# One PSUM pool with single 2-bank slots, mixed chunk sizes, and side work placed at fractions of each pass

## The chip, the cores and the metric

The kernel runs on one core of a Trainium2 chip. The metric is device time in microseconds; the time before is the median of three runs, 275.36 us (274.27 to 275.84). A profile of one execution (275.36 us, span 273.3 us) is shown beside it. Engines are named as in the profile: PE (matrix engine), PEld (its weight loads), DVE (vector), ACT (scalar), POOL (the engine whose queue starts the input loads here), SP (the queue of the output stores).

## The reference

```python
for _ in range(5):                      # P: [batch, head, 8, 8]
    P = exp(P - max(P)); P = P / sum(P, axis=-1); P = P / sum(P, axis=-2)
k_sorted = einsum('bhij,bhjcd->bhicd', P, k_blocks)     # blocks of 96 tokens
v_sorted = einsum('bhij,bhjcd->bhicd', P, v_blocks)
attn = softmax(scale * q_block @ k_sorted_block.T)      # inside each block
x = (attn @ v_sorted_block), heads side by side         # 3072 tokens x 512
g = x @ w_gate; val = x @ w_val                         # 512 -> 1536
out = (g * sigmoid(g) * val) @ w_out                    # 1536 -> 512
```

There are 4 batches, 8 heads, 768 tokens (8 blocks of 96), head size 64.

## The kernel before

**Mixing.** The 8x8 mixing matrices of all heads are made first (L177 to L201). A block-diagonal matrix per batch, `rmix`, mixes k over the blocks and passes q through an identity, so one pair of matmuls per token position c mixes k and moves q (`kq_chunk`, L217; `kq_wide`, L406, for batch 0). The result lies in PSUM as `tkq` and is drained to `kqt`, transposed. v is first copied to `vch` (L107) and mixed per head column (`v_chunk` L229, `v_wide` L421, and `v_pair_chunk` L240 for batches 2 and 3 at once); `tv` is drained to `vt`. `drain` (L202) copies on DVE ("v") or ACT ("s").

**Units.** One unit is half of the blocks of one head pair: `qk` (L253) computes scores and their exp, `av` (L273) multiplies by v, takes the reciprocal of the sum and scales (`r_sb`, `st`), `xtr` (L291) transposes to `x_ps` and copies to `xt`, the feed-forward's input. A batch has eight units, four per half.

**Feed-forward.** There are 8 passes n of 384 tokens each (half a batch). For each of 12 columns m, `gate` (L306) does four matmuls, a tanh on ACT (`th_sb`) and a vector step (`gs_sb`), `value` (L321) four matmuls and a vector step (`h`). `outp` (L332) multiplies h of the pass before by `wo_sb`, in three parts of four matmuls, then a copy and a store by SP. `gate`, `value` and `outp` all take their PSUM bank under the tag `gen`.

**PSUM.** The prologue has a pool `wide` (L65): three 2-bank slots wa, wb, wc, one bank wd for warm-up matmuls and one bank we. After the first half of batch 0 it is closed, and a second pool opens (L458): `gen` with 3 banks, `att` with 3 banks (shared by qk, tkq, tv and x_ps), `av` with one 2-bank slot.

**What sets the order.** On PE and POOL the order is the program's own (a manual schedule); in the prologue also on DVE and ACT. After the prologue a scheduler orders DVE and ACT. `merge` (L480) interleaves a pass (`ffn`, L496) with side work (units of this or the next batch, mixing of the next batch): after each step of the pass it places side steps in proportion to costs that are written by hand, so that the side work is through at 0.85 of the pass. In a pass with k/q mixing the units come first and six double chunks of 8+8 columns follow them.

**Loads.** All inputs come through POOL's queue in this order: v, q and k of batch 0, six pairs of gate and value weights of 256 columns (`load_gv`, L103), k, q and v of batch 1, `wo_sb`; after the copies of batch 1's v, the loads of batches 2 and 3 (L506 to L513).

Of the kernel before, what the change touches and what calls it, by code (L numbers as in the profile page):

```python
# [17 lines left out]
def kernel(  # L18
# [46 lines left out]
    wide = tc.tile_pool(name="wide", bufs=1, space=bass.MemoryType.PSUM)  # L65
    psum = wide.__enter__()
# [67 lines left out]
    for m in range(0, DF, 256):  # L134
        load_gv(m, m + 256)
    load_k(1, 0, C)
    load_q(1, 0, C)
    load_v(1, 0, C)
# [31 lines left out]
    def pair_tile(name, slot):  # L170
        return psum.tile([128, 1024], FP32, name=name, tag=slot)

    def bank_tile(name, slot):
        return psum.tile([128, 512], FP32, name=name, tag=slot)

    p_ps = pair_tile("p_ps", "wa")[0:BH, 0:NB * NB].rearrange("p (i j) -> p i j", j=NB)
# [40 lines left out]
    def kq_chunk(b, cb, eng, tag):  # L217
        nat = kq_tiles[b]
        dst = kqt_tile(b).rearrange("p (n c) -> p n c", c=C)
        rm = rmix[b].rearrange("p two a g i -> p two (a g i)")  # L220
        tp = psum.tile([128, 8, 2 * GI], FP32, name="tkq", tag=tag)
        for lc in range(8):
            for two in range(2):
                nc.tensor.matmul(tp[two * D:(two + 1) * D, lc, :],  # L224
                                 lhsT=nat[:, cb * 8 + lc, :],
                                 rhs=rm[:, two, :], start=True, stop=True)
        drain(eng, dst[:, :, ts(cb, 8)], tp.transpose([0, 2, 1]))

    def v_chunk(b, db, eng, tag):  # L229
        rows = highr if b % 2 else lowr  # L230
        dst = vt_tile(b // 2)[:, b % 2]
        mix = vmix[b // 2][rows, b % 2].rearrange("p a b -> p (a b)")
        tp = psum.tile([128, 8, H * NB], FP32, name="tv", tag=tag)
        for ld in range(8):
            at = (db * 8 + ld) * C
            nc.tensor.matmul(tp[:, ld, :], lhsT=vch[rows, at:at + 128], rhs=mix,  # L236
                             start=True, stop=True)
        drain(eng, dst[:, :, ts(db, 8)], tp[0:C].transpose([0, 2, 1]))

    def v_pair_chunk(pair, db, eng, tag):  # L240
        dst = vt_tile(pair).rearrange("p u n e -> p (u n) e")
        mix = vmix[pair].rearrange("p u a b -> p (u a b)")
        tp = psum.tile([128, 4, 2 * H * NB], FP32, name="tv", tag=tag)
        for ld in range(4):
            at = (db * 4 + ld) * C
            nc.tensor.matmul(tp[:, ld, :], lhsT=vch[:, at:at + 128], rhs=mix,  # L246
                             start=True, stop=True)
        drain(eng, dst[:, :, ts(db, 4)], tp[0:C].transpose([0, 2, 1]))
# [4 lines left out]
    def qk(b, u):  # L253
        half, g = divmod(u, H2)
        flat = kqts[b]
        pss = [psum.tile([128, 4, C], FP32, name=f"qk{two}", tag="att") for two in range(2)]
        for i4 in range(4):
            at = (g * NB + half * 4 + i4) * C
            for two in range(2):
                lo = two * D  # L260
                nc.tensor.matmul(pss[two][:, i4, :], lhsT=flat[lo:lo + D, at:at + 128],  # L261
                                 rhs=flat[lo:lo + D, GI * C + at:GI * C + at + C],
                                 start=True, stop=True)
        mine = []
        for two in range(2):
            e = e_all[:, ecount[0] % 8, :]
            ecount[0] += 1
            nc.scalar.activation(e[:, 0:4 * C], pss[two][0:C].rearrange("p a c -> p (a c)"),  # L268
                                 AF.Exp, scale=scale)
            mine.append(e)  # L270
        es[(b, u)] = mine

    def av(b, u, tag="av"):  # L273
        half, g = divmod(u, H2)
        vt = vts[b // 2][:, b % 2].rearrange("p (h i) e -> p h i e", h=H)
        av_ps = psum.tile([128, 2, 512], FP32, name="av_ps", tag=tag, bufs=1)
# [14 lines left out]
    def xtr(b, u, eng, tag="att"):  # L291
# [4 lines left out]
        x_ps = psum.tile([128, 4, C], BF16, name="x_ps", tag=tag, bufs=1 if tag == "we" else 3)  # L296
# [3 lines left out]
        drain(eng, xts[(b, half)][:, g, :], x_ps.rearrange("p a b -> p (a b)"))  # L300
# [5 lines left out]
    def gate(n, m):  # L306
        xt = xts[divmod(n, 2)]
        if m == 0:
            h_tiles[n] = hpool.tile([128, NFC, TW], BF16, name=f"h{n}", tag="h")
        g_ps = psum.tile([128, TW], FP32, name="g_ps", tag="gen")  # L310
        for kc in range(NKC):
            nc.tensor.matmul(g_ps, lhsT=wg_sb[:, kc, ts(m, 128)], rhs=xt[:, kc, :],  # L312
                             start=(kc == 0), stop=(kc == NKC - 1))
        th_sb = gsp.tile([128, TW], BF16, name="th_sb", tag="th")
# [6 lines left out]
    def value(n, m):  # L321
        xt = xts[divmod(n, 2)]
        v_ps = psum.tile([128, TW], FP32, name="v_ps", tag="gen")
        for kc in range(NKC):
            nc.tensor.matmul(v_ps, lhsT=wv_sb[:, kc, ts(m, 128)], rhs=xt[:, kc, :],  # L325
                             start=(kc == 0), stop=(kc == NKC - 1))
        nc.vector.scalar_tensor_tensor(h_tiles[n][:, m, :], v_ps, 0.5, gs_tiles.pop(m),  # L327
# [4 lines left out]
    def outp(n, t3, part):  # L332
        b, half = divmod(n, 2)
        h_w = h_tiles[n]
        if part == 0:
            o_tiles[n] = psum.tile([128, DM], FP32, name="o_ps", tag="gen")
# [11 lines left out]
    idle_ps = bank_tile("idle_ps", "wd")  # L348

    def fill(n, width=512):  # L350
        for _ in range(n):
            nc.tensor.matmul(idle_ps[:, 0:width], lhsT=warm_sb[:, 0:128], rhs=warm_sb[:, 0:width],
                             start=True, stop=True)

    for _ in range(84):
# [3 lines left out]
                     rhs=v_tiles[0][lowr, HC:HC + 2, :].rearrange("p c d -> p (c d)"),  # L359
                     start=True, stop=True)  # L360
    fill(9)

    w_ps = bank_tile("w_ps", "we").rearrange("p (s i b h) -> p s i b h", s=2, b=B, h=H)

    def weights(half):
        for i in range(NB):
            nc.tensor.matmul(w_ps[half * R:(half + 1) * R, half, i].rearrange("p b h -> p (b h)"),
# [6 lines left out]
    def mix_of(b):  # L374
# [5 lines left out]
            w_ps[lo:lo + R, b % 2, :, b].transpose([0, 2, 1]), op=ALU.mult)  # L380
# [3 lines left out]
            w_ps[0:R, 0, :, b].rearrange("p i (g two) -> p two g i", two=2), op=ALU.mult)  # L384

    def qk_wide(u):
        half, g = divmod(u, H2)
        flat = kqts[0]
        ps = pair_tile("qk", ["wa", "wb", "wc", "wc"][u]).rearrange("p (two n) -> p two n", two=2)
        for i4 in range(4):  # L390
            at = (g * NB + half * 4 + i4) * C
            for two in range(2):
                lo = two * D
                nc.tensor.matmul(ps[:, two, i4 * C:(i4 + 1) * C], lhsT=flat[lo:lo + D, at:at + 128],
                                 rhs=flat[lo:lo + D, GI * C + at:GI * C + at + C],
                                 start=True, stop=True)
        n = ecount[0] % 8
        ecount[0] += 2
        nc.scalar.activation(e_all[:, n:n + 2, 0:4 * C], ps[0:C, :, 0:4 * C], AF.Exp, scale=scale)  # L399
        es[(0, u)] = [e_all[:, n, :], e_all[:, n + 1, :]]  # L400

    mix_of(0)
    kdst = kqt_tile(0).rearrange("p (n c) -> p n c", c=C)
    rm = rmix[0].rearrange("p two a g i -> p two (a g i)")

    def kq_wide(cb, engs, slot):  # L406
        tp = pair_tile("tkq", slot).rearrange("p (l n) -> p l n", n=2 * GI)
        for lc in range(16):
            for two in range(2):
                nc.tensor.matmul(tp[two * D:(two + 1) * D, lc, :],  # L410
                                 lhsT=kq_tiles[0][:, cb * 16 + lc, :],
                                 rhs=rm[:, two, :], start=True, stop=True)
        w = 16 // len(engs)
        for n, eng in enumerate(engs):
            drain(eng, kdst[:, :, cb * 16 + n * w:cb * 16 + (n + 1) * w],
                  tp[:, n * w:(n + 1) * w].transpose([0, 2, 1]))

    vdst = vt_tile(0)[:, 0]
    vm = vmix[0][lowr, 0].rearrange("p a b -> p (a b)")

    def v_wide(db, eng, slot):  # L421
        tp = pair_tile("tv", slot).rearrange("p (l n) -> p l n", n=H * NB)
        for ld in range(16):
            at = (db * 16 + ld) * C
            nc.tensor.matmul(tp[:, ld, :], lhsT=vch[lowr, at:at + 128], rhs=vm,
                             start=True, stop=True)
        drain(eng, vdst[:, :, ts(db, 16)], tp[0:C].transpose([0, 2, 1]))

    for b in range(1, B):
        mix_of(b)  # L430
    slots = ["wa", "wb", "wc"]
    for n in range(4):
        v_wide(n, "s", slots[2 * n % 3])
        kq_wide(n, "v", slots[(2 * n + 1) % 3])
    kq_wide(4, "s", slots[8 % 3])
    kq_wide(5, "sv", slots[9 % 3])
    fill(3)
    qk_wide(0)
    qk_wide(1)
    qk_wide(2)  # L440
    av(0, 0, "wa")
    av(0, 1, "wb")
    xtr(0, 0, "s", "we")
    av(0, 2, "wa")
    qk_wide(3)
    fill(1)
    xtr(0, 1, "s", "we")
    av(0, 3, "wb")
    fill(1)
    xtr(0, 2, "s", "we")  # L450
    fill(2)
    xtr(0, 3, "s", "we")
    fill(2)
# [3 lines left out]
    wide.__exit__(None, None, None)  # L457
    psum = ctx.enter_context(tc.tile_pool(name="psum", bufs=3, space=bass.MemoryType.PSUM))  # L458
    man = tc.manual_schedule(engines={ET.PE, ET.Pool})
    man.__enter__()  # L460

    def units(b, us):
        todo = []
        us = list(us)
        for n in range(len(us) + 2):
            if n < len(us):
                todo.append((0.27, lambda u=us[n]: qk(b, u)))
# [92 lines left out]
```

The softmax here doesn't subtract the row's maximum and nothing guards it: scores larger than these inputs give would overflow.

## Time and profile before

| what | value |
|---|---|
| median of three runs | 275.36 us |
| profiled execution | 275.36 us |
| its span | 273.3 us |
| PE, DVE, ACT busy | 254.0, 163.8, 125.9 us |
| first group of pass 0 starts | 29.64 us |
| last output matmul group ends | 269.3 us |

The difference of 2.06 us between time and span lies around the profiled instructions. Page section 2 cuts the span into 40 slices of 6.8 us; a digit is the busy share in tenths. A table of stretches gives busy time and instruction count of each engine, then the mean clock granted to PE (1.00 is full), the DMA engines' share and GB/s. The waits list says which engine stood idle before which line, and for whom: total, count, longest.

### The profile page before, as it was taken

The numbers are of one execution on the slowest core, as the hardware profiler recorded it, in microseconds if no ns is written. First come the engines' busy times: TensorE is split into PE (matmuls) and PEld (weight loads), VectorE is DVE, ScalarE is ACT, GpSimd is POOL, SyncE is SP. The second block draws the span as 40 slices with busy tenths as digits, with TensorE's granted clock in tenths as the row PEclk, the third lists the DMA queues.
The fourth block names the chain that finished last, engine by engine and source line by source line (L and its number), as shares of the span: only waits on it lengthen the run. The fifth ranks groups of instructions, "written<-read, shape, count | busy, mean of one in ns | idle before, by whom it ended". The sixth has DMA issues, their size and how long they took to land.

```text
span 273.3 us, 6511 instructions
## 1 busy us (share of the span) xinstructions
PE 254.0 (93%) x2775; PEld 147.0 (54%) x2775; DVE 163.8 (60%) x362; ACT 125.9 (46%) x242; POOL 47.2 (17%) x46
## 2 busy tenths in 40 slices
PE   3786984999998999999999999999999999999994
PEld 3374452665555556556655556555555555555541
DVE  6685493675369488456359487466566766566500
ACT  3876631446752534439963435335332534323311
POOL 7766300793029300000000000000000000000000
PEclk9998898899999999999999999999999999999998
DMA  6979999909996101101101101101110111011122
GB/s 114 209 98 171 197 224 200 183 4 193 210 232 138 41 1 41 41 2 38 41 0 42 38 0 41 41 4 38 41 38 2 38 38 41 1 41 38 40 77 77
DMA packets 12700, 20.86 MB, mean 76 GB/s; under 512 B 896, under 2 KB 8576, under 8 KB 12032
## 3 DMA queue, kind: packets, MB, share of 16 engines
q0 software_dynamic: 9168, 14.16, 29.4%
q1 hardware_dynamic: 3504, 6.30, 6.2%
q8 instruction: 21, 0.34, 0.5%
q14 instruction: 7, 0.06, 0.1%
HBM read 28.32 MB, written 6.29 MB: 127 GB/s over the span
## 4 chain that ended last, share of the span: by engine, by line
PE 78%; DMA 13%; DVE 3%; POOL 3%; issue 1%; ACT 1%; ACTq 0%; POOLq 0%
PE o_ps L339 23%; PE v_ps L325 22%; PE g_ps L312 21%; DMA kq<-in_q_dram 6%; PE tkq L224 4%; DMA kq<-in_k_dram 4%; DMA wv_sb<-in_moe_w_val_dram 3%; PE qk L261 2%; PE av_ps L281 2%; PE x_ps L298 1%; PE tv L246 1%; PE tv L236 1%; DVE h L327 1%; DVE gs_sb L317 1%; POOL wg_sb L101 1%
## 5 line engine op out<-in xcount | busy, mean ns | idle before, releaser
L317 DVE SCALAR_TENSOR_TENSOR gs_sb<-th_sb,g_ps 128x384 bf16<-128x384 bf16 x96 | 53.0, 552 | 64.0 <-ACT th_sb L315 62.4
L312 PE MATMUL g_ps<-xt,wg_sb 128*128 128x384 bf16 x384 | 78.9, 328 | 0.1
L325 PE MATMUL v_ps<-xt,wv_sb 128*128 128x384 bf16 x384 | 78.9, 328 | 0.0
L315 ACT ACTIVATE th_sb<-g_ps 128x384 bf16<-128x384 f32 x96 | 47.5, 495 | 58.2 <-PE g_ps L312 57.3
L339 PE MATMUL o_ps<-wo_sb,h 128*128 128x512 bf16 x288 | 68.6, 379 | 0.0
L327 DVE SCALAR_TENSOR_TENSOR h<-v_ps,gs_sb 128x384 bf16<-128x384 f32 x96 | 53.3, 555 | 7.8 <-PE v_ps L325 0.6
L312 PEld LDWEIGHTS <-wg_sb 128*128 128x128 bf16 x384 | 34.7, 98 | 22.8 <-issue 1.4
L325 PEld LDWEIGHTS <-wv_sb 128*128 128x128 bf16 x384 | 34.0, 98 | 20.3 <-issue 0.3
L339 PEld LDWEIGHTS <-h 128*128 128x128 bf16 x288 | 26.5, 98 | 27.5
L344 ACT COPY o_sb<-o_ps 128x512 f32<-128x512 f32 x24 | 14.1, 587 | 54.4 <-PE o_ps L339 54.3
L114 POOL COPY vch<-v 64x1536 bf16<-64x1536 bf16 (+1 forms) x10 | 28.0, 2856 | 33.4 <-DMA v<-in_v_dram 33.4
L268 ACT ACTIVATE e_all<-qk 96x384 bf16<-96x384 f32 x56 | 24.3, 488 | 5.7 <-PE qk L261 5.6
L206 ACT CAST vt<-tv 96x512 bf16<-96x512 f32 (+1 forms) x28 | 21.8, 808 | 6.5 <-PE tv L236 3.4
L204 DVE CAST kqt<-tkq 128x512 bf16<-128x512 f32 (+1 forms) x23 | 17.9, 778 | 8.2 <-PE tkq L224 6.4
L287 DVE TENSOR_TENSOR st<-av_ps,r_sb 96x512 bf16<-96x512 f32 x32 | 21.9, 684 | 0.7
L206 ACT CAST kqt<-tkq 128x512 bf16<-128x512 f32 (+1 forms) x20 | 12.1, 604 | 11.4 <-PE tkq L224 10.7
L224 PE MATMUL tkq<-rmix,kq 128*64 128x64 bf16 x576 | 12.9, 200 | 3.6 <-DMA kq<-in_q_dram 3.6
L224 PEld LDWEIGHTS <-kq 128*64 128x64 bf16 x576 | 10.9, 115 | 9.8 <-issue 9.8
L281 PEld LDWEIGHTS <-e_all 96*128 96x128 bf16 x256 | 12.0, 99 | 7.5 <-ACT e_all L399 1.7
L281 PE MATMUL av_ps<-vt,e_all 96*128 96x65 bf16 x256 | 13.7, 195 | 2.0 <-ACT e_all L399 1.2
L298 PEld LDWEIGHTS <-st 96*128 96x128 bf16 x128 | 8.9, 100 | 8.1 <-DVE st L287 3.7
L298 PE MATMUL x_ps<-ident,st 96*128 96x96 bf16 x128 | 11.2, 211 | 2.1 <-DVE st L287 2.1
(59 smaller groups left out, 121.8 us busy)
## 6 DMA issues: line engine op xcount, KB each, us to landing
out_dram<-o_sb SPq DMA_DIRECT2D x24, 256.0 KB, 2.0
kq<-in_q_dram POOLq DMA_DIRECT2D x4, 768.0 KB, 13.2
kq<-in_k_dram POOLq DMA_DIRECT2D x3, 768.0 KB, 13.1
v<-in_v_dram POOLq DMA_DIRECT2D x3, 768.0 KB, 17.7
wg_sb<-in_moe_w_gate_dram POOLq DMA_DIRECT2D x6, 256.0 KB, 9.5
wv_sb<-in_moe_w_val_dram POOLq DMA_DIRECT2D x6, 256.0 KB, 10.0
wo_sb<-in_moe_w_out_dram POOLq DMA_DIRECT2D x1, 1536.0 KB, 24.2
v<-in_v_dram POOLq DMA_DIRECT2D x2, 384.0 KB, 5.6
```

Source lines behind the costliest of these rows:

```text
L114: eng.tensor_copy(dst, src.transpose([0, 2, 1]))
L206: nc.scalar.copy(dst, src)
L224: nc.tensor.matmul(tp[two * D:(two + 1) * D, lc, :], lhsT=nat[:, cb * 8 + lc, :], rhs=rm[:, two, :], start=True, stop=True)
L268: nc.scalar.activation(e[:, 0:4 * C], pss[two][0:C].rearrange("p a c -> p (a c)"), AF.Exp, scale=scale)
L281: nc.tensor.matmul(o[:, two, i4, :], lhsT=e[:, i4 * C:i4 * C + 128], rhs=vt[:, 2 * g + two, half * 4 + i4, :], start=True, stop=True)
L298: nc.tensor.transpose(x_ps[:, i4, :], st[:, i4].rearrange("p a b -> p (a b)"), ident[0:C, 0:C])
L312: nc.tensor.matmul(g_ps, lhsT=wg_sb[:, kc, ts(m, 128)], rhs=xt[:, kc, :], start=(kc == 0), stop=(kc == NKC - 1))
L315: nc.scalar.activation(th_sb, g_ps, AF.Tanh, scale=0.5)
L317: nc.vector.scalar_tensor_tensor(gs_sb, th_sb, 1.0, g_ps, op0=ALU.add, op1=ALU.mult)
L325: nc.tensor.matmul(v_ps, lhsT=wv_sb[:, kc, ts(m, 128)], rhs=xt[:, kc, :], start=(kc == 0), stop=(kc == NKC - 1))
L327: nc.vector.scalar_tensor_tensor(h_tiles[n][:, m, :], v_ps, 0.5, gs_tiles.pop(m), op0=ALU.mult, op1=ALU.mult)
L339: nc.tensor.matmul(o_ps, lhsT=h_w[:, m, ts(t3, 128)], rhs=wo_sb[:, m, :], start=(m == 0), stop=(m == NFC - 1))
```

## The change

The two pools become one of fixed slots: `gen` with 3 banks, `a` and `b` with one 2-bank slot each, `x` with one bank. `av` takes `a`; `qk`, `kq_chunk`, `v_chunk` and `v_pair_chunk` take `b` after the prologue; `x_ps` takes `x`. Chunks take a start and a size: 16 k/q columns in two banks, 16 v columns, 8 paired v columns, each drained by one instruction, on DVE and ACT in turn. `qk` does one exp over both banks. In the prologue, chunks of 8 and 16 columns go round all slots; the mixing matrices of batches 1 to 3 are made from a copy of `w_ps` in SBUF, behind the chunks. The first three groups of pass 0 (gate 0, value 0, gate 1) are taken apart by input row and placed among the last transposes of the prologue. The sixth pair of gate and value weights is loaded behind k and q of batch 1. `merge` places each side step at a fraction of the pass that is written down.

```diff
-    for m in range(0, DF, 256):
+    for m in range(0, 1280, 256):
         load_gv(m, m + 256)
     load_k(1, 0, C)
     load_q(1, 0, C)
+    load_gv(1280, DF)
     load_v(1, 0, C)
...
+    def bank_tile(name, tag="gen"):
+        return psum.tile([128, 512], FP32, name=name, tag=tag, bufs=3 if tag == "gen" else 1)
...
+    def kq_chunk(b, at, n, eng, tag):
...
+        tp = chunk_tile("tkq", n // 8, tag).rearrange("p (l n) -> p l n", n=2 * GI)
...
+        drain(eng, dst[:, :, at:at + n], tp.transpose([0, 2, 1]))
...
-        pss = [psum.tile([128, 4, C], FP32, name=f"qk{two}", tag="att") for two in range(2)]
+            wide = pair_tile("qk", tag).rearrange("p (two n) -> p two n", two=2)
...
+            nc.scalar.activation(e_all[:, n:n + 2, 0:4 * C], wide[0:C, :, 0:4 * C], AF.Exp, scale=scale)
...
-        av_ps = psum.tile([128, 2, 512], FP32, name="av_ps", tag=tag, bufs=1)
+        av_ps = pair_tile("av_ps", tag).rearrange("p (two n) -> p two n", two=2)
...
-        x_ps = psum.tile([128, 4, C], BF16, name="x_ps", tag=tag, bufs=1 if tag == "we" else 3)
+        x_ps = psum.tile([128, 4, C], BF16, name="x_ps", tag="x")
...
-                     rhs=v_tiles[0][lowr, HC:HC + 2, :].rearrange("p c d -> p (c d)"),
+                     rhs=v_tiles[0][lowr, 0:2, :].rearrange("p c d -> p (c d)"),
                      start=True, stop=True)
-    fill(9)
+    fill(idle_ps, 11)
...
+    mix_of(0, w_ps)
+    w_sb = const.tile([128, NB, B, H], FP32)
+    nc.scalar.copy(w_sb, w_ps)
+    v_chunk(0, 0, 8, "v", "gen")
+    v_chunk(0, 8, 16, "s", "a")
+    kq_chunk(0, 0, 16, "v", "b")
+    v_chunk(0, 24, 8, "s", "x")
+    v_chunk(0, 32, 8, "v", "gen")
+    v_chunk(0, 40, 16, "s", "a")
+    kq_chunk(0, 16, 16, "v", "b")
+    v_chunk(0, 56, 8, "s", "x")
+    kq_chunk(0, 32, 8, "v", "gen")
+    kq_chunk(0, 40, 16, "s", "a")
+    kq_chunk(0, 56, 16, "v", "b")
+    kq_chunk(0, 72, 8, "s", "x")
+    kq_chunk(0, 80, 8, "s", "gen")
+    kq_chunk(0, 88, 8, "v", "gen")
+    for b in range(1, B):
+        mix_of(b, w_sb)
...
+    qk(0, 0, "a")
+    qk(0, 1, "b")
+    qk(0, 2, "gen")
+    fill(idle_ps, 1)
+    av(0, 0, "a")
+    fill(idle_ps, 1)
+    av(0, 1, "b")
+    fill(idle_ps, 1)
+    x0 = xtr(0, 0)
+    qk(0, 3, "gen")
+    drain("s", *x0)
+    av(0, 2, "a")
+    av(0, 3, "b")
+    drain("s", *xtr(0, 1))
+    drain("s", *xtr(0, 2))
...
+    early((0, 1), (0, 1))
+    drain("v", *xtr(0, 3))
+    early((2,), (0, 1))
+    early((0, 1, 2), (2,))
+    early((3,))
+    gate_out(0, 0, first[0][0])
+    value_out(0, 0, first[1][0])
+    gate_out(0, 1, first[2][0])
...
+    def spread(steps, lo, hi):
+        return [(lo + (hi - lo) * n / len(steps), f) for n, f in enumerate(steps)]
...
-        return [(0.75, lambda cb=cb: two(cb)) for cb in range(0, 12, 2)]
+        return [lambda n=n: kq_chunk(b, n * 16, 16, "vs"[n % 2], "b") for n in range(6)]
...
+            while k < len(side) and side[k][0] * total <= done:
+                side[k][1]()
...
+    merge(ffn(0), spread(units(0, range(4, 8)), 0.0, 0.6) + spread(kqs(1), 0.65, 1.0))
+    merge(ffn(1), spread([lambda n=n: v_chunk(1, n * 16, 16, "sv"[n % 2], "b") for n in range(4)], 0.4, 0.6)
+          + spread(units(1, range(4)), 0.6, 0.97))
...
+    merge(ffn(2), spread(units(1, range(4, 8)), 0.0, 0.45) + spread(kqs(2), 0.45, 0.95))
+    merge(ffn(3), spread([lambda n=n: v_pair_chunk(1, n * 8, 8, "sv"[n % 2], "b") for n in range(8)], 0.0, 0.5)
+          + spread(units(2, range(4)), 0.5, 0.95))
+    merge(ffn(4), spread(units(2, range(4, 8)), 0.0, 0.45) + spread(kqs(3), 0.45, 0.95))
+    merge(ffn(5), spread(units(3, range(4)), 0.0, 0.9))
+    merge(ffn(6), spread(units(3, range(4, 8)), 0.0, 0.9))
```

## The prediction

> **What bounds the kernel now.** I read the page first (engines' shares and slices), then the stretches cut at the eight feed-forward passes, then the waits, then the timeline around each wait.
>
> ```profile
> PE 254.0 (93%) x2775; PEld 147.0 (54%) x2775; DVE 163.8 (60%) x362; ACT 125.9 (46%) x242; POOL 47.2 (17%) x46
> PE   3786984999998999999999999999999999999994
> PEclk9998898899999999999999999999999999999998
> ```
>
> TensorE (PE) is full from slice 8 on; only the first 50 us have holes. The pass boundaries (first gate of a pass to the next) are from the timeline; columns are length, then busy time and count of each engine, then clock, DMA share and GB/s:
>
> ```profile
> 29.60:59.45 29.85, 25.20 (x369) 15.30 (x370) 19.46 (x40) 12.15 (x26) 11.92 (x7) 0.94 0.98 170
> 59.45:90.54 31.09, 30.38 (x278) 16.62 (x277) 18.16 (x38) 15.11 (x31) 14.78 (x11) 1.00 0.79 170
> 90.54:121.79 31.25, 31.18 (x405) 18.14 (x404) 21.26 (x42) 13.97 (x29) 0.66 (x1) 1.00 0.08 27
> 121.79:152.92 31.13, 30.54 (x278) 18.50 (x277) 17.36 (x36) 20.92 (x39) 0.00 (x0) 1.00 0.07 27
> 152.92:184.17 31.25, 31.18 (x405) 18.14 (x404) 21.27 (x42) 13.97 (x29) 0.00 (x0) 1.00 0.07 27
> 184.17:210.97 26.80, 26.80 (x213) 15.11 (x212) 16.99 (x36) 10.57 (x23) 0.00 (x0) 1.00 0.08 31
> ```
>
> Pass 0 alone has a hole (4.6 us); passes 2, 4, 5, 6 and 7 have none. The waits name it, and the clock after it shows a second cost:
>
> ```profile
> PE tkq L224 <- DMA kq<-in_q_dram: 3.6, 1, 3.6
> PE x_ps L298 <- DVE st L287: 2.1, 4, 0.7
> 43.00:46.40 3.40, 1.21 (x36) 0.96 (x37) 0.48 (x1) 0.59 (x1) 0.00 (x0) 0.98 1.01 205
> 46.40:49.80 3.40, 3.40 (x41) 1.88 (x40) 1.84 (x4) 1.08 (x2) 0.40 (x1) 0.52 1.21 197
> ```
>
> Batch 1's q lands at 45.06 us; PE waits 3.6 us, then runs 3.4 us at half clock (1.7 us lost).
>
> **PE prices**, start to start in the timeline: gate or value group 0.655 us; output part 0.865; qk 0.27 plus 0.10 to switch to it; av 0.26; transposes 0.17; mixing of 16 k/q columns 0.63 plus 0.09; 4 paired v columns 0.22. Check: pass 2 = 24x0.655 + 9x0.865 + 4x0.80 + 6x0.72 = 31.0 against 31.25. So a pass has a floor, and what counts is the waits put on top.
>
> **Vector and scalar prices.** An instruction's full duration sets when it releases a slot; the next one starts earlier:
>
> ```profile
> 84.07 0.54 DVE L317 SCALAR_TENSOR_TENSOR gs_sb<-th_sb,g_ps 128x384 bf16<-128x384 bf16 x1
> 84.53 0.35 DVE L204 COPY xt<-x_ps 128x384 bf16<-128x384 bf16 x1
> 84.80 0.54 DVE L327 SCALAR_TENSOR_TENSOR h<-v_ps,gs_sb 128x384 bf16<-128x384 f32 x1
> ```
>
> So VectorE (DVE): gs or h 0.55, next after 0.46; st 0.69/0.60; xt 0.35/0.27. By shape, a two-bank drain takes 1.22 us on DVE and 1.01 to 1.06 on ScalarE (ACT), a wide exp 0.80, a tanh 0.49. A two-bank drain of v on DVE is not in the trace: by its elements 1.22; bounds 1.06 (ACT's) and 1.37 (two one-bank drains).
>
> **The Trainium skill.** "Perfetto Trace Analysis", Optimizing Scalar/DVE Operations: the write-acknowledge half of an instruction overlaps the next; the trace agrees (0.55 long, 0.46 apart). The same page, Matmuls: independent groups should rotate through PSUM banks so that draining one overlaps the next; agreed, pass 2 with three attention banks has no idle PE. "TensorE: Matmul & The Clock Gate", What's actually happening: a sparse 3.4 us window brings half clock; the trace agrees (0.52 after the wait). "DMA: Bandwidth & Descriptors", Two DMAs through the same engine are not ordered: descriptors of one queue start in order; the trace fits, with loads landing one after the other.
>
> **The change, part by part.** All walks follow the instruction order that the built program has on each engine.
>
> *Loads.* On POOL's queue k and q of batch 1 pass the last gate/value pair (two of 256 KB); v and wo keep their places. At 205 GB/s 512 KB are 2.6 us: q lands at about 42.5, the pair at 45. Mixing of batch 1 is now first wanted at 44.1 (below), those weights at 49: neither waits. That removes 3.6 + 1.7 us.
>
> *Prologue.* The gate matmul now waits for the first half of v (6.2 instead of 8.1 us), so the weight matmuls come at 11.5 instead of 12.2; the first k mixing still waits for its load (13.86, as before). Drains split over both engines: DVE has v 0.69, then from 14.6 three of 1.22 and three of 0.69 with 0.4 of waiting, done 20.4; ACT done 20.0 (before: 21.73). The copy to w_sb (about 0.4, ACT idle there; 0.4 if not) costs nothing; the six mix steps (6x0.21) move behind the last drain, under qk and exp. From qk at 20.5: exps end 21.7, 22.5, 23.5; st 23.1, 24.0; the fourth unit's exps 24.8; then the single x slot is drained on ACT at 25.3, 26.2, 27.1. Twelve early matmuls (2.0 us) and the last transposes end at 28.5, full clock. Before, the thin stretch up to 25.9 gave half clock until 29.3; the same adds 1.4. I take 29.4 (28.5 to 30.2), with three groups done; before, the first group started at 29.64.
>
> *Pass 0, floor* 21x0.655 + 3.2 + 4.3 = 21.25. *Waits*: the first value group waits for a gate's slot, 1.0; second qk for the exp of the first (slot b is single) 0.2; fourth av 0.2; last transposes for the x slot, whose drain stands behind st, 0.9. Mixing, counted from the early end (29.4): each chunk needs b drained by its predecessor's reader, DVE and ACT in turn. Gate 8 ends at 14.6, chunk 0 at 15.35; on DVE gs of that gate comes first (tanh 0.2 after the gate for 0.5, gs 15.3 to 15.9), the drain runs 15.8 to 17.0. PE has one value group to do (to 16.0), then chunk 1 stands until 17.05: 1.0. Its drain on ACT is over before chunk 2 comes. Chunk 2 (19.1 to 19.7) is drained behind gs and h of the groups before it, 20.15 to 21.4; PE wants chunk 3 at 20.5: 0.95. Chunks 4 and 5 have one group in front and wait 0.4 (ACT) and 0.6 (DVE). Together 5.2. PE is in order: behind a waiting chunk stand the next gate and its tanh, gs and h, so nothing fills the hole. End 29.4 + 26.5 = 55.9 against 59.45: -3.55.
>
> *Pass 1*: 24x0.655 + 9x0.865 + 3.2 + 4x0.72 = 29.6; two v chunks wait 0.4 and 0.5 for b, one qk 0.25, x slot 0.1: 30.8 against 31.1, -0.3. POOL's copies of v end at 60.7; the first v chunk comes at 65.8.
>
> *Passes 2 and 4*: floor 31.0; the second qk waits 0.35 (exp of the first stands behind a tanh and ends 1.35 after that qk started, PE has 0.92 to do); the last transposes wait 0.9 (the copy out of x runs 13.6 to 13.95 behind st and h, PE is there at 13.1): +1.0 each. The mixing is three groups apart there: no wait.
>
> *Pass 3*: paired v in 8 columns (0.44): floor 15.7 + 7.8 + 3.2 + 8x0.44 = 30.2. Every second chunk is drained on DVE, behind a gs that itself waits for its tanh: chunk 1 is written at 2.85, gs ends 3.65, the drain 4.8 (later if chunk 0's ACT drain is late); PE wants chunk 2 at 4.1: 0.85. After chunk 3 the same gives 0.5. The drain of chunk 7 (15.5 to 16.7) stands before an h in DVE's queue; that h holds a slot of the three general ones until 17.2, and a gate waits 0.9 for it. Second qk 0.4, x slot 0.7: 33.5, +2.4. Before, these drains were all ACT's, 16 of 0.8, and PE waited for none.
>
> *Passes 5 to 7 and the tail*: steps 1.8 us apart, 0.
>
> Sum: -3.55 - 0.3 + 1.0 + 2.4 + 1.0 = +0.55. Profiled execution 273.3 + 2.06 around = 275.36, which is the median too; after: 273.85 + 2.06 = **275.9**. The change trades one DMA stall for many short slot waits (12.3 us of them).
>
> **Rivals.**
> *A, slower: the DVE queue in front of each release is longer.* If instructions follow each other at full duration (0.55, 0.69), my walks give passes 0 to 4 1.1, 0.8, 0.35, 0.5, 0.35 more: 3.1, so 279.0. For: waits on x and b come in bursts, and DVE is already busy 21.3 of 31.25 us. Against: the overlap in the timeline. It decides from a quarter on (276.7).
> *B, faster: a third of the slot waits isn't there*, because engines reach the drains as PE ends: -4.1, 271.8. For: DVE is busy only 56 to 68% in passes 1 to 4, and the old passes 2 and 4 show none. Against: the order in the queues is fixed, and the third bank is gone. From -2.0 it counts as faster.
> *C, the earlier load doesn't do its work*: q still lands at 45.06: 1.0 us more of wait in pass 0, 276.9. Against: 205 GB/s hold from 39.6 to 46.4 with nothing else in the queue.
>
> **Chances.** Forecast 0.41 (274.4 to 277.4), A 0.27 (277.4 to 280.5), B 0.25 (270.5 to 273.9), C 0.07. Half a per cent (1.4 us) is about what a measurement tells from no change. Faster 0.25; slower A, a fifth of the forecast (above 276.7) and half of C: 0.39; same 0.36. Range: 272.2 to 279.4 leaves out a third each of A and B, with the v drain's bounds (some three waits by 0.15 us) and those of the prologue's end (0.9) inside; the forecast's own range is 274.4 to 277.4.
>
> **What would show it.** Right: no PE wait on q; pass 0 ends near 56; PE waits on DVE and ACT of 0.3 to 1.0 us before tkq, tv, x_ps and av_ps, in passes 0 to 4 only; pass 3 the longest at 33.5. Wrong: passes 2 to 4 at 31.2 (B), or waits over 1 us and pass 0 past 57 (A); a half-clock window inside passes 0 to 4 is outside my sum.

## The result: 1.35% slower, and where the time went

The changed kernel takes 279.07 us (median of four runs, 277.53 to 279.26) against 275.47 us before (median of four): a ratio of 1.0135, 95% interval 1.0094 to 1.0177. The forecast was 275.9 us, within half a per cent of no change. The time lies inside the stated range, 272.2 to 279.4, but outside the forecast's own, 274.4 to 277.4. The profiled execution took 279.09 us with a span of 276.7 us, 3.4 us more than the span of before.

The page of the changed kernel (engine shares, then PE's busy tenths and granted clock in 40 slices of 6.9 us):

```profile
PE 254.5 (92%) x2750; PEld 149.8 (54%) x2772; DVE 169.7 (61%) x362; ACT 115.5 (42%) x190; POOL 47.2 (17%) x46
...
PE   3898898789899989999989898999999999999994
...
PEclk9959799999999999999999999999999999999999
```

PE is as busy as before, ACT has 52 instructions less and 10 us less work, DVE 6 us more. The new things are the 5 and the 7 in the clock row (slices 3 and 5, from 14 to 21 and from 28 to 35 us), and the 8s in PE's row past slice 13, where before had only 9s.

The same kernel's stretches, cut at the ends of the passes (length, busy time and count of PE, PEld, DVE, ACT and POOL, clock, DMA share, GB/s):

```profile
31.93:58.86 26.93, 22.14 (x358) 13.82 (x357) 20.18 (x41) 11.09 (x19) 11.35 (x5) 1.00 0.96 172
58.86:89.49 30.63, 29.62 (x275) 16.95 (x277) 20.14 (x39) 12.59 (x21) 14.56 (x11) 1.00 0.80 173
89.49:121.74 32.25, 31.09 (x403) 18.17 (x404) 20.36 (x39) 13.54 (x22) 0.00 (x0) 1.00 0.07 27
121.74:155.29 33.55, 31.32 (x275) 18.71 (x277) 21.55 (x40) 15.22 (x23) 0.00 (x0) 1.00 0.07 24
155.29:187.56 32.27, 31.12 (x402) 18.20 (x404) 20.34 (x39) 13.54 (x22) 0.00 (x0) 1.00 0.07 26
187.56:214.21 26.65, 26.49 (x211) 15.09 (x213) 17.01 (x36) 10.54 (x19) 0.00 (x0) 1.00 0.08 31
```

| stretch | before | forecast | after |
|---|---|---|---|
| prologue, to the end of what it holds of pass 0 | 29.6 | 29.4 | 31.93 |
| pass 0, rest | 29.85 | 26.5 | 26.93 |
| pass 1 | 31.09 | 30.8 | 30.63 |
| pass 2 | 31.25 | 32.25 | 32.25 |
| pass 3 | 31.13 | 33.5 | 33.55 |
| pass 4 | 31.25 | 32.25 | 32.27 |
| passes 5 to 7 and tail | 89.1 | 89.1 | 89.1 |

Passes 2 to 4 lose 4.4 us, as forecast. Passes 0 and 1 gain 3.4 us in length where 3.65 were forecast. The prologue, which now holds three groups of pass 0 too, was to take no longer; it takes 2.3 us more than before, 2.5 more than forecast. That one line is nearly all of the miss in span.

In passes 0 to 4, PE's waits are of the kinds forecast. Those of over 0.4 us in total (total, count, longest):

```profile
PE x_ps L304 <- DVE xt L204: 2.8, 4, 0.8
PE tkq L226 <- DVE kqt L204: 2.6, 3, 1.1
PE qk L267 <- ACT e_all L276: 0.9, 4, 0.2
PE v_ps L334 <- DVE gs_sb L326: 0.8, 1, 0.8
PE g_ps L316 <- DVE h L339: 0.6, 1, 0.6
PE tv L248 <- DVE vt L204: 0.6, 2, 0.4
```

All of these but qk's end with an instruction of DVE, an engine that is 61% busy. Three smaller ones are left out here: two end with ACT (0.4 before tv, 0.3 before tkq), one with DVE (0.3 before tv). None is for q: the single 3.6 us wait is gone. In all PE stands idle for 10.3 us in these passes, where 12.3 us of waits were forecast.

The prologue of the kernel before in finer stretches, in the same columns:

```profile
10.50:14.00 3.50, 3.04 (x46) 1.58 (x46) 2.06 (x11) 2.15 (x3) 1.36 (x1) 1.00 1.01 197
14.00:17.00 3.00, 2.88 (x128) 2.71 (x124) 2.77 (x4) 2.33 (x3) 1.17 (x3) 1.00 0.22 41
17.00:20.00 3.00, 2.34 (x108) 2.03 (x103) 2.45 (x3) 2.48 (x3) 3.00 (x5) 1.00 1.10 134
```

The same stretches of the changed kernel:

```profile
10.50:14.00 3.50, 2.34 (x43) 1.46 (x42) 2.25 (x8) 2.83 (x4) 1.69 (x1) 1.00 1.02 199
14.00:17.00 3.00, 2.98 (x72) 2.85 (x74) 1.82 (x2) 1.58 (x3) 1.00 (x3) 0.52 0.23 42
17.00:20.00 3.00, 3.00 (x104) 2.85 (x102) 1.82 (x2) 1.77 (x3) 3.00 (x5) 0.50 0.92 118
```

Read the second number together with its count. From 14 to 20 us, PE of the changed kernel looks full (5.98 us busy) with 176 matmuls; before did 236 in 5.22 us. It is full because each takes longer: the clock is 0.5. A chunk of 32 mixing matmuls shows it; first before, then changed (start, duration):

```profile
13.86 0.69 PE L410 MATMUL tkq<-rmix,kq 128*64 128x64 bf16 x32 [0.15 <-DMA kq<-in_k_dram]
16.77 1.07 PE L226 MATMUL tkq<-rmix,kq 128*64 128x64 bf16 x32
```

Just ahead, from 10.5 to 14 us, PE is busy 2.34 of 3.5 us where before had 3.04.

### The profile page after: what moved, and what is told of

The parts are those of the page before. It is cut to its first block, busy times and chain, and to the rows that moved or that the text cites. A ratio compares the mean times of both kernels' runs of the same rounds, so it can differ in the third digit from the quotient of the medians.

```text
span 276.7 us, 6431 instructions
## 1 busy us (share of the span) xinstructions
PE 254.5 (92%) x2750; PEld 149.8 (54%) x2772; DVE 169.7 (61%) x362; ACT 115.5 (42%) x190; POOL 47.2 (17%) x46
## 4 chain that ended last, share of the span: by engine, by line
PE 76%; DVE 10%; ACT 7%; issue 3%; DMA 2%; ACTq 0%; DVEq 0%; POOLq 0%
PE o_ps L351 22%; PE g_ps L316 19%; PE v_ps L334 19%; PE tkq L226 5%; PE qk L267 3%; DVE gs_sb L326 3%; ACT th_sb L324 3%; PE av_ps L287 2%; PE x_ps L304 2%; DVE h L339 2%; DMA v<-in_v_dram 2%; DVE vt L204 2%; PE tv L238 2%; ACT e_all L276 2%; ACT vch L111 2%
## 5 line engine op out<-in xcount | busy, mean ns | idle before, releaser
L334 PE MATMUL v_ps<-xt,wv_sb 128*128 128x384 bf16 x380 | 77.6, 326 | 0.8 <-DVE gs_sb L326 0.8
L316 PE MATMUL g_ps<-xt,wg_sb 128*128 128x384 bf16 x376 | 76.6, 326 | 0.6 <-DVE h L339 0.6
L351 PE MATMUL o_ps<-wo_sb,h 128*128 128x512 bf16 x268 | 67.3, 379 | 1.3 <-DVE h L339 0.2
L334 PEld LDWEIGHTS <-wv_sb 128*128 128x128 bf16 x380 | 33.5, 97 | 21.0 <-issue 1.1
L276 ACT ACTIVATE e_all<-qk 96x768 bf16<-96x768 f32 x30 | 24.0, 802 | 14.3 <-PE qk L267 14.2
L226 PEld LDWEIGHTS <-kq 128*64 128x64 bf16 x768 | 16.0, 121 | 9.3 <-issue 9.1
L226 PE MATMUL tkq<-rmix,kq 128*64 128x64 bf16 x768 | 17.9, 206 | 3.2 <-DVE kqt L204 2.6
L204 DVE CAST kqt<-tkq 128x1024 bf16<-128x1024 f32 (+1 forms) x14 | 15.8, 1143 | 7.5 <-PE tkq L226 7.5
L291 DVE RECIPROCAL r_sb<-av_ps 96x8 f32<-96x8 f32 x32 | 6.4, 200 | 19.1 <-PE av_ps L287 19.0
L206 ACT CAST kqt<-tkq 128x1024 bf16<-128x1024 f32 (+1 forms) x12 | 11.2, 942 | 10.3 <-PE tkq L226 10.3
## 6 DMA issues: line engine op xcount, KB each, us to landing
wo_sb<-in_moe_w_out_dram POOLq DMA_DIRECT2D x1, 1536.0 KB, 24.7
```

The costliest lines, as they stand in the source:

```text
L226: nc.tensor.matmul(tp[two * D:(two + 1) * D, lc, :], lhsT=kq_tiles[b][:, at + lc, :], rhs=rm[:, two, :], start=True, stop=True)
L276: nc.scalar.activation(e_all[:, n:n + 2, 0:4 * C], wide[0:C, :, 0:4 * C], AF.Exp, scale=scale)
L351: nc.tensor.matmul(o_ps, lhsT=h_w[:, m, ts(t3, 128)], rhs=wo_sb[:, m, :], start=(m == 0), stop=(m == NFC - 1))
```

## The experiments

Theories: (1) the slot waits of passes 0 to 4 are DVE's queue in front of each drain, and moving the drain takes them away; (2) the prologue's loss is the half clock, brought by thin PE work; (3) the earlier load is what saves pass 0. The rivals stand with each run. Ratios are to the kernel before, run on the same chip; the intervals are 95%. The runs were on three chips, so two rows are compared by their ratios.

| run | median us | ratio | interval |
|---|---|---|---|
| changed kernel, again | 278.55 | 1.0142 | 1.0106 to 1.0178 |
| before, k and q earlier | 275.63 | 1.0033 | 1.0008 to 1.0058 |
| before, k, q and v earlier | 272.93 | 0.9924 | 0.9894 to 0.9954 |
| changed, load order undone | 277.96 | 1.0128 | 1.0101 to 1.0155 |
| changed, first fills as before | 279.13 | 1.0122 | 1.0079 to 1.0166 |
| changed, fills in two gaps | 276.68 | 1.0095 | 1.0062 to 1.0127 |
| changed, x copies on ACT | 273.90 | 0.9966 | 0.9945 to 0.9988 |
| changed, paired v on ACT | 275.71 | 1.0036 | 1.0017 to 1.0055 |
| changed, x and v on ACT | 272.47 | 0.9929 | 0.9903 to 0.9955 |
| changed, k/q drains halved | 276.92 | 1.0104 | 1.0080 to 1.0129 |
| x, v and the fills | 270.78 | 0.9864 | 0.9837 to 0.9891 |
| the same, pass 0 k/q on ACT, more fills | 269.48 | 0.9828 | 0.9794 to 0.9862 |

### The changed kernel again

> The changed kernel unaltered, as a control beside the three variants on one chip: 278 to 279 us, with the same waits (3.2 us before tkq in pass 0). Theory (the slot waits and the prologue's half clock make the loss): about 1.2% above the kernel before. If it comes out within 0.5% of before, half of the loss was chance of the clock windows.

1.0142, and the profile shows the same waits and the same half clock. The loss repeats.

### Only the earlier loads, in the kernel before

```diff
-    for m in range(0, DF, 256):
+    for m in range(0, 1280, 256):
         load_gv(m, m + 256)
     load_k(1, 0, C)
     load_q(1, 0, C)
+    load_gv(1280, DF)
     load_v(1, 0, C)
```

> The kernel before with one part of the change alone: k and q of batch 1 go ahead of the sixth pair of gate and value weights on POOL's queue; nothing else. If the loads land one after the other at 205 GB/s, q lands 2.6 us earlier (42.5 instead of 45.06); the first mixing of batch 1, wanted at 41.5, waits 1.0 us instead of 3.6, and no half-clock window follows: 3.6 - 1.0 + 1.7 = 4.3 us less, 271.2 us. Rival: q's landing doesn't move with its place in the queue (or the half-clock window comes all the same, from another sparse stretch): 0 to 2.6 us less, 273 to 275.5.

1.0033: the gain isn't there. PE's longest wait in passes 0 and 1 of this run, and the stretch behind it:

```profile
PE tv L237 <- POOL vch L114: 3.1, 1, 3.1
61.47:64.88 3.41, 3.38 (x20) 1.66 (x21) 0.61 (x2) 1.16 (x2) 3.06 (x6) 0.50 0.71 123
```

PE no longer waits for q. Pass 1 begins earlier (56.88, before 59.45), and its first v chunk then stands until POOL has copied batch 1's v; 3.4 us at half clock follow, and pass 1 takes 35.8 us for 31.1. The profiled execution is the slowest of the 22 (278.12 us): its prologue ran at half clock, and pass 0 began at 32.20 instead of 29.64, which by itself hides part of any wait for q. The next two runs ask whether that is the whole story, and whether the load order does anything in the changed kernel.

### k, q and v earlier, in the kernel before

```diff
     load_q(1, 0, C)
-    load_gv(1280, DF)
     load_v(1, 0, C)
+    load_gv(1280, DF)
```

> The kernel before with k, q and v of batch 1 all loaded ahead of the sixth gate/value pair. Theory (with k and q alone moved, pass 1 began earlier and stood 3.1 us for POOL's four copies of v, which gave the saving back): v lands 2.6 us earlier, its copies end near 59, the wait in pass 1 falls to 0.5 or less, and the saving shows: about 2.5 us under the run with k and q alone, 272.0 to 273.5. Rival (what is given back is lost in the clock windows, not in the wait for v): 275 to 276 again.

0.9924: v's load alone, moved by one more pair, gives 1.1% (1.0033 to 0.9924). POOL's copies in the run with k and q alone (start, duration, and last what it waited for):

```profile
50.23 11.22 POOL L114 COPY vch<-v 64x1536 bf16<-64x1536 bf16 x4 [17.49 <-DMA v<-in_v_dram]
```

And in this one:

```profile
46.12 11.25 POOL L114 COPY vch<-v 64x1536 bf16<-64x1536 bf16 x4 [13.13 <-DMA v<-in_v_dram]
```

The copies begin 4.1 us earlier, end at 57.4, and no PE wait on `vch` is left. So the old kernel's hole was worth 2 us by its loads alone, once both stages behind the weights were served.

### The load order undone, in the changed kernel

> The changed kernel with the loads in the order of the kernel before (the sixth gate/value pair ahead of k and q of batch 1). Theory: placed at 0.65 of pass 0, the first k/q chunk comes at 46.8 us, after q has landed in either order (about 45 undone), so the load order is worth nothing in this schedule: no PE wait on q, within 0.5 us of the changed kernel, 278 to 279 us. Rival (the load order carries part of the saving, as the prediction had it): a wait on q of 0.5 us or more before the first chunk and 1 us or more slower, 279.5 to 281.

1.0128 against 1.0142 and 1.0135: nothing. There is no wait on q, which landed at 44.98; the first chunk comes at 47.54 in this run (its line, start and duration first):

```profile
47.54 0.70 PE L225 MATMUL tkq<-rmix,kq 128*64 128x64 bf16 x32
```

So the 3.6 us wait is gone without the new load order: the mixing comes later, through its place at 0.65 of the pass, and through the late prologue of this kernel. Pass 0 began near 32.6 here; had it begun at 29.4 as forecast, the chunk would come near 44.3 and wait 0.7 us (an estimate from these figures). In the run with x, v and the fills below it comes at 42.92, with q landed at 41.55. In the old order, with q near 45, that would be a wait of about 2 us (an estimate; not run). So the load order is worth nothing in this kernel as it ran; in the faster ones below, by this estimate, it is worth something.

### The first fills as before

```diff
-                     rhs=v_tiles[0][lowr, 0:2, :].rearrange("p c d -> p (c d)"),
+                     rhs=v_tiles[0][lowr, HC:HC + 2, :].rearrange("p c d -> p (c d)"),
-    fill(idle_ps, 11)
+    fill(idle_ps, 9)
```

> The changed kernel with the warm-up of the kernel before (the gate matmul waits for the second half of v, nine wide fills instead of eleven). Theory: in the profiled run of the changed kernel PE ran at half clock from 14.1 to 20.9 us because the fills end at 11.3 and leave a sparse window; with the fills ending at 12.1 the mixing of batch 0 runs at full clock, the first qk starts about 1.5 to 2 us earlier (20.7 instead of 22.7), 277.3 us. Rival: [...] the half-clock stretch comes from the thin stretch itself, wherever the fills end: no change, 278 to 279.5.

1.0122: no change, a miss. Mixing ran at half clock again in the profiled execution, so beginning the warm-up as before is not enough to prevent it. PE still stood idle for 0.38 us before the first v chunk and 0.64 before the first k/q chunk.

### Fills in the two gaps

```diff
+    fill(idle_ps, 2)
     v_chunk(0, 0, 8, "v", "gen")
     v_chunk(0, 8, 16, "s", "a")
+    fill(idle_ps, 1)
     kq_chunk(0, 0, 16, "v", "b")
```

> Two 512-column warm-up matmuls between the weights and the first v chunk and one before the first k/q chunk, in the 0.53 and 0.32 us in which PE stands idle there. Theory (the thin stretch from 10.7 to 14.1 us is what gives the half clock in mixing of batch 0): mixing at full clock, first qk at 20.7 instead of 22.7, end of the early groups 30.0 instead of 31.9, 1.5 to 2 us under the changed kernel. Rival (the small matmuls of mixing count as a thin stretch themselves): the half clock comes all the same, no change.

1.0095, with a median 1.9 us under the changed kernel on the same chip. With six executions each the two intervals overlap, so it is the profile that tells the two apart. The prologue's stretches in this run:

```profile
14.00:17.00 3.00, 2.72 (x112) 2.57 (x113) 2.18 (x3) 2.31 (x4) 0.71 (x2) 1.00 0.26 49
17.00:20.00 3.00, 2.02 (x112) 1.84 (x112) 2.69 (x3) 2.26 (x3) 3.00 (x5) 1.00 0.78 99
...
26.00:29.00 3.00, 2.43 (x18) 1.51 (x18) 1.10 (x3) 0.96 (x2) 1.46 (x3) 0.69 1.45 195
```

From 14 to 20 us these are 224 matmuls instead of 176, at full clock, and PE even waits for drains. The first qk comes at 21.31 (22.66 in the changed kernel). A half-clock stretch still hits the early groups here, which end at 30.8 instead of 31.9. All three profiled runs with these fills mixed at full rate; all eight of the changed prologue without them ran at least one k/q chunk at half rate, the second at the latest.

### Copies out of x on ACT

```diff
-                todo.append(lambda u=us[n - 2]: drain("v", *xtr(b, u)))
+                todo.append(lambda u=us[n - 2]: drain("s", *xtr(b, u)))
```

> The changed kernel with the copies out of the x slot on ACT instead of DVE in all passes. Theory: the last transposes of passes 0, 2, 3 and 4 wait 0.5 to 0.8 us (as PE's idle time) because the single x slot's copy stands in DVE's queue behind st and h; on ACT, which is less busy there, the copy comes at once: 0.6 us less in each of four passes, and DVE is relieved of 28 copies: 2.5 us less, 276.5 us. Rival: st itself is late, so the transposes wait for DVE all the same: under 0.6 us less, 278.5 or more.

0.9966, more than expected. First the wait in pass 2 of the changed kernel, as its timeline shows it (start, duration, engine; the lines in between are of the tanh and of PE):

```profile
101.81 0.34 PE L304 MATMUL x_ps<-ident,st 96*128 96x96 bf16 x4
...
102.09 0.68 DVE L293 TENSOR_TENSOR st<-av_ps,r_sb 96x512 bf16<-96x512 f32 x1
102.69 0.54 DVE L339 SCALAR_TENSOR_TENSOR h<-v_ps,gs_sb 128x384 bf16<-128x384 f32 x1
...
103.16 0.34 DVE L204 COPY xt<-x_ps 128x384 bf16<-128x384 bf16 x1
...
103.55 0.33 PE L304 MATMUL x_ps<-ident,st 96*128 96x96 bf16 x4 [0.76 <-DVE xt L204]
```

The transposes end at 102.15, but their copy (0.34 us long) starts at 103.16: st and h stand ahead of it on DVE. The next transposes need the same bank and lose 0.76. With the copy on ACT, passes 2 to 4 are:

```profile
86.60:118.19 31.59, 31.11 (x402) 18.10 (x404) 19.34 (x35) 15.07 (x26) 3.15 (x2) 1.00 0.08 27
118.19:151.03 32.84, 31.15 (x275) 18.64 (x277) 20.62 (x36) 16.89 (x27) 0.00 (x0) 1.00 0.07 25
151.03:182.62 31.59, 31.11 (x403) 18.10 (x405) 19.34 (x35) 15.07 (x26) 0.00 (x0) 1.00 0.07 27
```

That is 0.66, 0.71 and 0.68 us less; with 0.80 in pass 0 and 0.08 in pass 1 the edit gives 2.9 us, where 2.5 was expected. Another 2.0 us of this profiled run lie in the prologue (early groups end at 29.9), where the edit changes nothing.

### Paired v on ACT

```diff
-    merge(ffn(3), spread([lambda n=n: v_pair_chunk(1, n * 8, 8, "sv"[n % 2], "b") for n in range(8)], 0.0, 0.5)
+    merge(ffn(3), spread([lambda n=n: v_pair_chunk(1, n * 8, 8, "s", "b") for n in range(8)], 0.0, 0.5)
```

> The changed kernel with all eight drains of paired v in pass 3 on ACT. Theory: the waits in pass 3 (0.6 us for b in two places, 0.6 us of a gate for an h) come from drains of 1.2 us in DVE's queue between gs and h; on ACT pass 3 goes from 33.55 to about 32.3: 1.2 us less, 277.8 us. Rival: the single b slot sets the pace whichever engine drains it, since ACT takes about 1.2 us for a chunk as well and has a tanh in front: pass 3 stays at 33.2 to 33.8, 279 us.

1.0036. Pass 3 of this run, all other passes being as in the changed kernel within 0.1 us:

```profile
121.56:153.48 31.92, 31.02 (x275) 18.77 (x277) 17.36 (x36) 19.59 (x27) 0.00 (x0) 1.00 0.07 26
```

33.55 becomes 31.92: the waits before tv and before a gate are gone, though ACT's drain takes nearly as long (1.18 us) as DVE's (1.22). So it is the queue that counts: the drain no longer stands in DVE's, and h, with the general bank that it frees, no longer stands behind the drain.

### Both on ACT

> The copies out of the x bank and the drains of paired v both on ACT. Theory (the two kinds of waits are separate, each in front of a DVE queue): the gains add, passes 2 and 4 at 31.6, pass 3 at 31.2 or below, 4.0 us under the changed kernel, 271.5 to 273.5 us and below the kernel before. Rival (both put ACT in front of the same tanh, so that ACT becomes what is late in pass 3): pass 3 stays above 32, and the time is that of the x variant alone, 273.9.

0.9929. Pass 3 is 31.22, 2.33 us shorter, and the two single runs gave 0.71 and 1.63: they add up, so the waits are separate. PE's waits of over 0.4 us in passes 0 to 4 of this run:

```profile
PE tkq L226 <- DVE kqt L204: 2.6, 3, 1.1
PE qk L267 <- ACT e_all L276: 0.9, 4, 0.2
PE v_ps L334 <- DVE gs_sb L326: 0.8, 1, 0.8
```

### Half a k/q drain on each engine

```diff
-        drain(eng, dst[:, :, at:at + n], tp.transpose([0, 2, 1]))
+        if b == 0:
+            drain(eng, dst[:, :, at:at + n], tp.transpose([0, 2, 1]))
+        else:
+            drain("s", dst[:, :, at:at + 8], tp[:, 0:8].transpose([0, 2, 1]))
+            drain("v", dst[:, :, at + 8:at + 16], tp[:, 8:16].transpose([0, 2, 1]))
```

> Each k/q chunk of batches 1 to 3 is drained by two instructions, half on ACT and half on DVE at once, instead of one engine for the whole. Theory (PE waits because one 1.2 us drain stands behind gs and h in one queue): the 3.2 us of waits before tkq in pass 0 fall to about 2.0, passes 2 and 4 stay, 1.2 us under the changed kernel. Rival (the queue in front is the wait, not the drain's length): every chunk now has DVE's queue in front of it, waits of 0.5 before all five, no change or 0.5 us slower.

The median is 1.0104, but the passes say what the edit did. Pass 0 of this run:

```profile
29.30:55.96 26.66, 22.20 (x357) 13.88 (x356) 20.41 (x43) 12.07 (x22) 8.46 (x5) 1.00 1.11 192
```

PE's wait on DVE's k/q drains in it:

```profile
PE tkq L226 <- DVE kqt L204: 2.6, 4, 0.6
```

Three waits of up to 1.1 us have become four of up to 0.6, with the same sum. The 0.3 us wait on ACT's drain is gone, which is what the pass gained (0.27 us); the others are unchanged. The forecast fall to 2.0 didn't come, and the rival's picture fits: with half of every drain in DVE's queue, four of the five later chunks wait for that queue. The rest of the median can't come from the edit, which touches nothing before 44 us; in this profiled run the early groups ended at 29.3.

The Trainium skill ("Perfetto Trace Analysis", Optimizing Scalar/DVE Operations) says that where these engines aren't saturated but make others wait, breaking up instructions may let work finish sooner. Here it hardly does (pass 0 goes from 26.93 to 26.66), as the half on DVE still stands in that queue; moving the whole drain does, in the last run below.

### x, v and the fills

Both edits on ACT and the three fills.

> Copies out of the x bank and paired-v drains on ACT, and the three warm-up matmuls in the prologue's gaps. Theory (three separate costs): mixing of batch 0 at full clock, passes as with x and v alone (26.1, 30.5, 31.6, 31.2, 31.6): 1 to 2 us under the kernel without the fills (272.5), 270.5 to 271.5. Rival (the drains in the prologue are what is late next and a later half-clock window takes the rest): 272.0 to 272.5.

0.9864. The early groups end at 28.8 in the profiled run (30.9 without the fills), the passes are as without the fills, within 0.1 us. The ratio falls from 0.9929 to 0.9864, and the intervals don't overlap: the fills' gain comes on top.

### And the k/q chunks of pass 0 on ACT

```diff
-    merge(ffn(0), spread(units(0, range(4, 8)), 0.0, 0.6) + spread(kqs(1), 0.65, 1.0))
+    merge(ffn(0), spread(units(0, range(4, 8)), 0.0, 0.6) + spread(kqs(1, "ss"), 0.65, 1.0))
...
+    thin(1)
     av(0, 3, "b")
     drain("s", *xtr(0, 1))
+    thin(3)
     drain("s", *xtr(0, 2))
```

(`thin` issues 384-column warm-up matmuls into the bank that the first gate fills afterwards.)

> As the one before, and the six k/q chunks of pass 0 all drained by ACT, and four more warm-up matmuls of 384 columns in the idle gaps of 0.2 and 0.6 us ahead of the early groups. Theory (PE waits for DVE's queue in front of the drain, 2.6 us in pass 0; ACT has only a tanh there): these waits fall to about 1.2, pass 0 from 26.1 to 24.7, and the early groups run at full clock (up to 1.5 us): 268.5 to 270. Rival (a drain by ACT for every chunk leaves bank b late for the next, and delays the tanh of the gate ahead, so DVE's gs and a gen bank): pass 0 stays at 25.8 or more, 270.5 to 271.5.

0.9828: 1.7% below the kernel before, the fastest run here. Its pass 0:

```profile
28.47:53.08 24.61, 22.06 (x357) 13.80 (x356) 15.83 (x34) 15.62 (x26) 6.60 (x5) 1.00 1.20 208
```

PE's waits before k/q chunks in it:

```profile
PE tkq L226 <- ACT kqt L206: 1.4, 4, 0.3
```

24.61 against 26.14 with the drains in turn, 24.7 expected. ACT and DVE now share pass 0 evenly (15.6 and 15.8 us). What the four extra fills add isn't told apart: the early groups already ran at full clock in the run before.

## Why the prediction missed

The measured 279.07 us lies inside the stated range, but that is luck: the upper part of the range stood there for longer DVE queues (A), and those are not what came. The end of the prologue had its own bounds, 28.5 to 30.2, and it came at 31.93.

*Prologue: wrong, and this decides.* The step took the end of mixing at 20.5 from the order of drains, and left PE's speed in mixing at that of the profile before. PE ran it at half clock: first qk at 22.66, +2.2 us, and the early groups, for which 1.4 us of half clock had been allowed, ended at 31.93 instead of 29.4. With fills in the gaps the same prologue reached its first qk at 20.6 to 21.3 and ended its groups at 28.5 to 30.8: the order of drains was judged nearly rightly. The prediction had applied the thin stretch to what follows the first qk, not to the mixing and the gaps in front of it (0.53 us before the first v chunk and 0.33 before the first k/q chunk).

*Loads: the fact right, the cause wrong.* There is no wait on q. But the saving of 3.6 + 1.7 us was given to the load order, and the run with it undone shows no wait either: the later place of the mixing, with a prologue as late as this one, does it alone. Alone in the old kernel the loads of k and q give nothing, since POOL's copies of v are late next.

*Pass 0*: 26.93 for 26.5. The three waits on DVE's k/q drains are 0.9, 1.1 and 0.6, those forecast 1.0, 0.95 and 0.6. *Pass 1*: 30.63 for 30.8. *Passes 2 and 4*: 32.25 and 32.27 for 32.25. *Pass 3*: 33.55 for 33.5, and this is luck: PE's own work was put at 30.2 us and takes 31.3, while the waits, put at 3.35 us, come to 2.2 (0.6 before the gate for 0.9). With nearly all of these waits gone, in the run with x and v on ACT, the pass still takes 31.22 us. Over passes 0 to 4 the same holds: 2.2 us more of work and 1.9 us less of waits nearly cancel. *Passes 5 to 7*: nothing, as said. The misses in span: 2.53 for the prologue, 0.43 for pass 0, -0.17 for pass 1, 0.07 for the rest, 2.86 us in all; 276.7 less the 273.85 forecast is 2.85.

*Rivals.* A had nearly this time (279.0) and is wrong: it asked for 3.1 us more of waits in passes 0 to 4, and these passes together are 0.3 us over the forecast, with fewer waits. B is half right: 1.9 of the 12.3 us of waits aren't there, where it asked for a third, but PE's longer work takes their place and the time it gave didn't come. C didn't come: q landed at 41.36.

*Open.* That the fills take the half clock out of mixing is shown; which stretch brings it isn't settled. PE's busy share from 10.5 to 14 us doesn't tell: with it at 2.50 (first fills as before) and 2.63 of 3.5 us (x copies on ACT) PE mixed slowly, with it at 2.53 and 2.40 (the first and the last run with fills) at full rate. Nor is there one cause for all slow prologues. In the run with the load order undone PE was slow ahead of the gaps already. Here are the 16 matmuls that bring the mixing matrices into PSUM, in the changed kernel and in that run:

```profile
11.54 0.77 PE L378 MATMUL w_ps<-ident,p_bf 32*64 32x32 bf16 x16 [0.28 <-DVE p_bf L196]
11.23 0.94 PE L377 MATMUL w_ps<-ident,p_bf 32*64 32x32 bf16 x16
```

In both runs with earlier loads in the old kernel, whose prologue is that of before, these matmuls took 0.84 and 0.85 us, where before took 0.57, and mixing was slow from its start: there the warm-up had not brought the full clock in time. So the profile of before showed the better case of its prologue. But a slow one need not show in the old kernel's time. PE came to the first k/q chunk of batch 1 at 41.6 us there and stood until q landed at 45.06; a prologue 2.6 us later fits into that wait (an estimate from these figures; not run). The changed kernel has no such wait, so the same half clock shows in full.

## What to carry to other kernels

When a slot is single, price each release from the queue in front of the draining engine: a 0.34 us copy behind two vector steps cost PE 0.76 us on an engine 61% busy, and moving it, not splitting it, gave the time back. When a wait is removed by an earlier transfer, ask at once who is late next, test whether the new placement would have removed it anyway, and ask what loss the wait had been hiding. A forecast for a thin stretch of matmuls needs both clocks: a profile shows the one that this execution had.

## What the hardware showed

The record of the granted clock can miss half-rate work. In the profiled run with k, q and v earlier, a stretch of mixing reads:

```profile
14.00:17.00 3.00, 3.00 (x85) 2.75 (x82) 1.71 (x4) 1.83 (x2) 0.83 (x2) 1.00 0.23 42
```

Its first k/q chunk, in the timeline:

```profile
14.17 1.07 PE L411 MATMUL tkq<-rmix,kq 128*64 128x64 bf16 x32
```

The clock column says 1.00, but the 32 matmuls take 1.07 us; in the profile before they took 0.69. The Trainium skill ("TensorE: Matmul & The Clock Gate", Seeing it yourself) says that the recorded clock events have been seen to be unreliable; this run agrees. The time of a known matmul is the surer sign.
